# Filling the Q ring of two head pairs by engine copies, and a new order of the first part, in a fused attention and feed-forward kernel

## Chip, cores and metric

The kernel runs on one core of a Trainium2 chip. The metric is the time of one execution on the device in microseconds. In the names of the profile, PE is TensorE (matrix products; PEld are its weight loads), DVE is VectorE, ACT is ScalarE, POOL is GpSimd and SP is SyncE, which here only issues DMAs.

## The reference

The work is a block-sparse causal attention followed by a feed-forward layer. There are 4 batches, 8 heads, 768 positions and a head size of 64.

```
chunk, top_k = 32, 6                      # 24 chunks of 32 keys
k_min, k_max = min and max of k over each chunk
ub  = sum_d max(q * k_min, q * k_max)     # bound of each query on each chunk
ub  = where(chunk is not in the future, ub, -1e9)
sel = the 6 chunks with the highest ub, for each query
scores = q @ k^T / 8, masked by sel and by causality
x   = softmax(scores) @ v                 # heads side by side: (4, 768, 512)
xn  = (x - mean) / sqrt(var + 1e-6) * g
out = x + relu(xn @ w1) @ w2              # hidden size 2048, float32 out
```

## The kernel before

The heads are taken in 16 pairs (numbered g, four for each batch): the two heads of a pair share the 128 partitions, one in the upper and one in the lower half. The 768 positions are six tiles of 128, in two halves of three tiles (r = 0 or 1).

Every step of the work is a small function. A text constant, ORDER, lists all calls by hand, 928 of them. Each engine executes its own instructions strictly in that order; there is no scheduler that could pull something ahead. A step is written as its name and its arguments: smm.5.0.0 is "scores of pair 5, half 0, bin 0". A suffix such as @1 or @2 picks another engine for a step that has several to choose from, or a number of extra products on constants for a step that has such (function busy).

The steps that matter, for a pair g:

- ld, ldb and ldv load q, k and v. Pairs 0 to 3 (batch 0) come in halves and are transposed on PE (turn, line 236); pairs 4 and up are loaded so that VectorE can transpose them (line 229).
- kbound (lines 283 and 284) takes minima and maxima of k by chunk, kdiag and bounds make the bounds, select picks the chunks, maskt and mring bring the mask into the ring.
- qhi and qlo split q in two f16 parts (lines 251 to 256); qrel makes the positive parts (262, 263).
- kcopy and qring write K and Q into ring tiles KA, KB, QA and QB (four of each, so that pair g uses tile g % 4). In one product these give the score and the mask penalty. For pairs 4 and up the Q part is a copy within the on-chip memory, issued as two DMAs of 96 KB from SyncE (lines 267 and 268).
- smm (line 414) are the score products, sexp (422) the exponentials on ScalarE, diag (429) cuts above the diagonal on GpSimd, values (445) multiplies with v, norm and pstat divide by the sum and gather the statistics. The score products write into a pool of two PSUM buffers, which the first feed-forward product shares.

For a batch b and a half r: centre (484 to 487) subtracts the mean, xt transposes by DMA (504), m1 (513) and relu (525) are the first feed-forward product, m2 (538) the second, fin (547, 552) adds x and stores. The weights come in four chunks each, w1 (173) and w2 (177), as DMAs that GpSimd issues and that convert to f16.

Products that compute nothing are there to keep TensorE busy: warm(n) issues n products of 512 columns on a zeroed tile while the first loads are under way (line 373); busy (line 117) issues some on constants ahead of the products of certain steps.

In the part around 60 us SyncE's queue is, in order, the loads of pairs 6 and 7 (ldb.6.kn, ldb.6.qn, ldb.7.kn, ldb.7.qn), then the ring of pair 5 (qring.5), then the transposes of the second half of batch 0 (xt.0.1).

Of the kernel before, what the change touches and what calls it, by code (L numbers as in the profile page):

```python
# [19 lines left out]
def kernel(  # L20
# [10 lines left out]
    nc = tc.nc  # L31
    P = nc.NUM_PARTITIONS
# [9 lines left out]
    HP = H // 2  # L42
# [39 lines left out]
    NK = 4  # L82
    QA = [ring.tile([P, S], F16, name=f"QA{i}", tag=f"QA{i}") for i in range(NK)]
# [24 lines left out]
    def pick(*engines):  # L108
        return engines[min(other[0], len(engines) - 1)]

    def copy(eng, o, i):
        return eng.copy(o, i) if eng is nc.scalar else eng.tensor_copy(o, i)
# [152 lines left out]
    def qring(g, i=None):  # L265
        if i is None:
            nc.sync.dma_start(QA[g % NK][0:64, :], st[g]["qh"][0:64, :])
            nc.sync.dma_start(QB[g % NK][64:P, :], st[g]["qh"][64:P, :])
            return
        qt = st[g]["qn", i]  # L270
        a, z = span(g, i)
        nc.scalar.activation(QA[g % NK][0:64, a * P:z * P], qt[0:64, :], ACTF.Copy, scale=QS)
        nc.scalar.activation(QB[g % NK][64:P, a * P:z * P], qt[64:P, :], ACTF.Copy, scale=QS)
# [269 lines left out]
    def fin(b, r, i, e=None):  # L543
# [13 lines left out]
        consts ld.0.0 rrows.0.0 rinit.0 ld.1.0 ld.2.0 warm.8 turn.0.qn.0 rrows.2.1@1 qpos.0.0 rrows.3.1 qring.0.0  # L557
        turn.0.kn.0 rinit.2 kbound.0.0 rinit.1 turn.1.qn.0 kcopy.0.0 ld.3.0 turn.1.kn.0 kbound.1.0 kdiag.0.0
        qring.1.0 rrows.1.0 rinit.3 turn.2.qn.0@3 ld.0.1 rrows.0.1 bounds.0.0@2 kdiag.1.0 rrows.1.1 qpos.1.0
        select.0.0 turn.2.kn.0 kcopy.2.0@1 kcopy.1.0 qpos.2.0 bounds.1.0@2 kbound.2.0 qring.2.0 maskt.0.0 select.1.0  # L560
        kdiag.2.0 turn.3.kn.0 mring.0.0@1 ld.1.1 turn.3.qn.0 kcopy.3.0 rrows.3.0 ldv.2.0 maskt.1.0 qpos.3.0
        kbound.3.0 smm.0.0.0 ldv.0.0 mring.1.0 bounds.2.0@2 select.2.0 turn.0.kn.1 qring.3.0 rrows.2.0 smm.0.0.1
        turn.1.kn.1 turn.0.qn.1 ld.2.1 kdiag.3.0 sexp.0.0.0 ldv.3.0 kcopy.0.1 qpos.0.1 kbound.1.1 sexp.0.0.1
        kbound.0.1 kcopy.1.1 ldv.1.0 kdiag.0.1 smm.1.0.0@2 bounds.3.0@2 maskt.2.0 diag.0.0 qring.0.1 bounds.0.1
        sexp.1.0.0 select.3.0 values.0.0 maskt.3.0 mring.2.0 kdiag.1.1 smm.1.0.1 select.0.1 smm.2.0.0 w1.2.3 w1.1.3
        w1.0.2 norm.0.0 sexp.1.0.1 ldb.4.qn smm.2.0.1 sexp.2.0.0 mring.3.0 maskt.0.1 ld.3.1 turn.1.qn.1 sexp.2.0.1
        qpos.1.1 ldb.5.kn mring.0.1 diag.1.0 values.1.0 norm.1.0 diag.2.0 pstat.0.0 smm.3.0.0 pstat.1.0
        turn.2.kn.1@1 sexp.3.0.0 kbound.2.1 qring.1.1 turn.4.qn smm.3.0.1@2 sexp.3.0.1 bounds.1.1 values.2.0
        smm.0.1.0 diag.3.0 select.1.1 kcopy.2.1 smm.0.1.2@1 values.3.0 sexp.0.1.0 norm.2.0 sexp.0.1.2 norm.3.0
        turn.2.qn.1 smm.0.1.1 pstat.2.0 sexp.0.1.1 kdiag.2.1@1 qpos.2.1 smm.0.1.3 qring.2.1 ldv.0.1 turn.3.kn.1  # L570
        maskt.1.1 pstat.3.0 qhi.4 kcopy.3.1 mring.1.1 diag.0.1 smm.1.1.0@2 ldb.4.kn bounds.2.1 sexp.1.1.0 sexp.0.1.3
        centre.0.0 xt.0.0.0 xt.0.0.1 select.2.1 turn.3.qn.1@3 kbound.3.1 qlo.4 smm.1.1.3 xt.0.0.2 ldb.5.qn qring.4
        maskt.2.1 turn.4.kn sexp.1.1.3 smm.1.1.2 values.0.1 kdiag.3.1 qpos.3.1 qrel.4 kbound.4 sexp.1.1.2 smm.1.1.1
        bounds.3.1 mring.2.1 sexp.1.1.1 w1.3.3 late select.3.1 kdiag.4 diag.1.1 norm.0.1 turn.5.kn m1.0.0.0 kcopy.4
        turn.5.qn relu.0.0.0 kbound.5 m1.0.0.4 ldv.1.1 qring.3.1 ldb.6.kn relu.0.0.4 w2.0.0 m1.0.0.2 relu.0.0.2
        bounds.4 pstat.0.1 m1.0.0.10 qhi.5 m1.0.0.6 relu.0.0.10 relu.0.0.6 maskt.3.1 kcopy.5@1 kdiag.5 m1.0.0.8
        m1.0.0.12 relu.0.0.8 m1.0.0.14 relu.0.0.12 ldb.6.qn smm.2.1.0 select.4 qlo.5 rstd.0.0 qrel.5 relu.0.0.14
        sexp.2.1.0 bounds.5 smm.2.1.1 smm.2.1.2 ldv.2.1 ldv.3.1 w2.1.0 turn.6.kn sexp.2.1.1 values.1.1 smm.2.1.3
        mring.3.1 diag.2.1 sexp.2.1.2 select.5 sexp.2.1.3 norm.1.1 smm.3.1.0 maskt.4 sexp.3.1.0 smm.3.1.2 kbound.6
        mring.4 maskt.5 w2.2.1 w2.3.1 sexp.3.1.2 smm.3.1.1 ldb.7.kn smm.3.1.3 sexp.3.1.1 ldb.7.qn values.2.1 qring.5  # L580
        sexp.3.1.3 mring.5 pstat.1.1 norm.2.1 smm.4.1.0 diag.3.1 sexp.4.1.0 smm.4.0.0 kdiag.6 values.3.1 m2.0.0.0.0
        norm.3.1 pstat.2.1 pstat.3.1 smm.5.0.0 kcopy.6 sexp.4.0.0 sexp.5.0.0 m2.0.0.2.0 m2.0.0.1.0 smm.4.0.1
        m2.0.0.0.1 sexp.4.0.1 turn.6.qn qhi.6 centre.0.1 qlo.6 smm.4.1.3 turn.7.kn smm.4.1.2 sexp.4.1.3 sexp.4.1.2
        m2.0.0.1.1 turn.7.qn qrel.6 smm.4.1.1 rstd.0.1 m2.0.0.2.1 kcopy.7 kbound.7 m2.0.0.0.2 m2.0.0.2.2 sexp.4.1.1
        m2.0.0.1.2 smm.5.1.0 xt.0.1.0 bounds.6 m2.0.0.2.3 select.6 xt.0.1.1 xt.0.1.2 ldb.8.kn sexp.5.1.0 qhi.7
        m1.0.1.0 qlo.7 diag.4.0 ldv.4 turn.8.kn qring.6 m1.0.1.6 relu.0.1.0 relu.0.1.6 m2.0.0.0.3 m1.0.1.14 ldb.8.qn
        kdiag.7 fin.0.0.0 qrel.7 fin.0.0.2 relu.0.1.14 ldb.9.qn diag.4.1 m1.0.1.2 kbound.8 maskt.6 ldv.5 relu.0.1.2
        ldv.6 kcopy.8 ldb.10.qn m2.0.0.1.3 qring.7 turn.8.qn mring.6 m1.0.1.4 relu.0.1.4 diag.5.0 m1.0.1.8 qhi.8
        relu.0.1.8 ldv.7 fin.0.0.1 values.4.0 norm.4.0 smm.5.0.1 bounds.7 qlo.8 smm.5.1.1 qrel.8 select.7 sexp.5.0.1
        kdiag.8 sexp.5.1.1 smm.5.1.3 values.4.1 diag.5.1 sexp.5.1.3 smm.5.1.2 ldb.9.kn values.5.0 ldb.10.kn  # L590
        ldb.12.qn sexp.5.1.2 smm.6.1.0 sexp.6.1.0 bounds.8 norm.4.1 smm.6.1.2 norm.5.0 values.5.1 sexp.6.1.2
        smm.6.1.1 sexp.6.1.1 pstat.4.1 m2.0.1.0.0 m1.0.1.10 qring.8 m1.0.1.12 m2.0.1.0.1 relu.0.1.10 relu.0.1.12
        smm.6.0.0 sexp.6.0.0 turn.9.qn maskt.7 select.8 smm.6.0.1 sexp.6.0.1 m2.0.1.0.2 pstat.4.0 maskt.8 smm.6.1.3
        qhi.9@1 diag.6.0 m2.0.1.0.3 mring.7 pstat.5.0 norm.5.1 fin.0.1.0 smm.7.0.0 diag.6.1 sexp.6.1.3 sexp.7.0.0
        smm.7.0.1 values.6.1 diag.7.0 values.6.0 mring.8 sexp.7.0.1 norm.6.1 smm.7.1.0 smm.7.1.2 values.7.0 qlo.9
        m2.0.1.2.0 norm.6.0 norm.7.0 sexp.7.1.0 smm.7.1.3 sexp.7.1.2 m2.0.1.1.0 pstat.6.0 pstat.7.0 smm.7.1.1
        ldb.11.kn sexp.7.1.3 m2.0.1.1.1 sexp.7.1.1 diag.7.1 turn.9.kn centre.1.0 xt.1.0.0 smm.8.1.0 m2.0.1.2.1
        sexp.8.1.0 smm.8.0.0 m2.0.1.2.2 kbound.9 m2.0.1.1.2 smm.8.1.2 m2.0.1.2.3 xt.1.0.2 kcopy.9 qrel.9 sexp.8.0.0
        values.7.1 sexp.8.1.2 smm.8.0.1 pstat.6.1 xt.1.0.1 smm.8.1.3 sexp.8.0.1 norm.7.1 sexp.8.1.3 kdiag.9 diag.8.1
        ldb.11.qn pstat.5.1 m2.0.1.1.3 smm.8.1.1 fin.0.1.2 bounds.9 pstat.7.1 centre.1.1 sexp.8.1.1 xt.1.1.0  # L600
        m1.1.0.0 m1.1.0.2 relu.1.0.0 xt.1.1.1 m1.1.0.4 relu.1.0.2 m1.1.0.6 relu.1.0.4 relu.1.0.6 m1.1.0.8 relu.1.0.8
        xt.1.1.2 m1.1.0.14 relu.1.0.14 m1.1.0.10 m1.1.0.12 relu.1.0.10 turn.10.qn relu.1.0.12 ldv.8 ldv.10 select.9
        turn.10.kn kbound.10 fin.0.1.1 maskt.9 m1.1.1.0 qhi.10@1 ldv.9 qring.9 kdiag.10 qlo.10 m1.1.1.4 rstd.1.0
        qrel.10 mring.9 kcopy.10 turn.11.kn values.8.1 bounds.10 select.10 relu.1.1.0 smm.9.0.0 turn.11.qn
        m2.1.0.0.0 norm.8.1 ldb.12.kn relu.1.1.4 smm.9.1.0 sexp.9.0.0 m2.1.0.0.1 smm.9.0.1 sexp.9.1.0 sexp.9.0.1
        kbound.11 m2.1.0.1.0 m2.1.0.0.2 diag.8.0 smm.9.1.3 sexp.9.1.3 m2.1.0.0.3 qhi.11 qring.10 ldv.13 maskt.10
        qring.11 mring.10 smm.9.1.2 sexp.9.1.2 values.8.0 smm.9.1.1 sexp.9.1.1 kdiag.11 m2.1.0.1.1 m1.1.1.14
        m2.1.0.1.2 kcopy.11 relu.1.1.14 fin.1.0.0 smm.10.0.0 ldv.11 qlo.11 m2.1.0.1.3 diag.9.1 qrel.11 turn.12.qn
        bounds.11 sexp.10.0.0 m1.1.1.2 m1.1.1.8 ldb.13.kn turn.12.kn relu.1.1.2 fin.1.0.1 select.11 rstd.1.1
        m1.1.1.6 relu.1.1.8@1 norm.8.0 maskt.11 values.9.1 mring.11 smm.10.0.1 relu.1.1.6 smm.10.1.0 qhi.12  # L610
        kbound.12 norm.9.1 sexp.10.0.1 m2.1.0.2.0 diag.9.0 smm.10.1.3 values.9.0 m2.1.0.2.1 sexp.10.1.0 smm.10.1.1
# [79 lines left out]
```

## Time and profile before

| | before |
|---|---|
| time, median of 3 runs | 288.89 us (288.71 to 291.12) |
| span of the profiled execution | 288.7 us, 6793 instructions |
| PE busy | 271.7 us (94%) |
| VectorE busy | 211.8 us (73%) |
| ScalarE busy | 180.8 us (63%) |
| GpSimd busy | 94.1 us (33%) |
| DMA | 32.42 MB, mean 112 GB/s |
| chain that ended last | PE 81%, DMA 8%, VectorE 7%, ScalarE 2% |

Busy shares are means over the whole span. The profile also gives them by 40 slices, with the TensorE clock that was granted, and by any stretch one asks for. The chain is followed back from the last instruction, at each step to what released it.

### The profile page before, as it was taken

What the parts mean: (1) busy time and instruction counts of PE and PEld (TensorE: products, weight loads), DVE (VectorE), ACT (ScalarE), POOL (GpSimd) and SP (SyncE); (2) the same over time, 40 slices, a digit from 0 to 9 for tenths busy, and PEclk for the clock granted to TensorE, in tenths of its full rate; (3) what the DMA queues carried; (4) which work ended last, traced back from release to release, by engine and by line L of the source; (5) the groups of instructions that cost most, each with busy time, mean ns of one, the idle gap of its engine ahead of it and who ended that gap; (6) DMA issues with size and microseconds to landing.
All of it is one profiled execution on the core that took longest, in us unless ns stands there. A gap on an engine that the chain in (4) does not pass through costs nothing.

```text
span 288.7 us, 6793 instructions
## 1 busy us (share of the span) xinstructions
PE 271.7 (94%) x2628; PEld 181.8 (63%) x2628; DVE 211.8 (73%) x629; ACT 180.8 (63%) x241; POOL 94.1 (33%) x165
## 2 busy tenths in 40 slices
PE   5999999992799999999899999999999999999994
PEld 2889997671355777566656776566667745555541
DVE  5699999998079998999699979998797483221212
ACT  3688999694185977865775877667777522513210
POOL 8505615781039203182442643141072200100100
PEclk9999999998599999999999999999999999999999
DMA  6999997999949989489919691927011112310102
GB/s 141 203 179 177 202 156 126 167 151 194 139 84 70 188 162 182 78 116 133 172 29 185 112 148 20 136 81 163 16 43 59 39 20 72 93 39 36 73 0 110
DMA packets 136063, 32.42 MB, mean 112 GB/s; under 512 B 127072, under 2 KB 132960, under 8 KB 136032
## 3 DMA queue, kind: packets, MB, share of 16 engines
q1 hardware_dynamic: 106640, 24.39, 43.7%
q0 software_dynamic: 29248, 7.34, 27.4%
q8 instruction: 20, 0.33, 0.5%
q10 hardware_dynamic: 144, 0.26, 0.4%
q14 instruction: 11, 0.09, 0.1%
HBM read 27.53 MB, written 6.29 MB: 117 GB/s over the span
## 4 chain that ended last, share of the span: by engine, by line
PE 81%; DMA 8%; DVE 7%; ACT 2%; issue 1%; ACTq 0%; DVEq 0%
PE yp L538 27%; PE mm L513 25%; PE mm L414 11%; PE sm L445 6%; DMA QA<-q 3%; PE ub L333 3%; DMA xT<-xc 3%; PE ub L320 2%; ACT pt L422 2%; PE tr L236 2%; DMA raw<-in_k_dram 2%; PE tr L117 2%; DVE xc L487 1%; PE trh L361 1%; PE ub L117 1%; PE mm L117 1%
## 5 line engine op out<-in xcount | busy, mean ns | idle before, releaser
L422 ACT ACTIVATE pt<-mm 128x1024 f16<-128x1024 f32 (+2 forms) x96 | 84.6, 917 | 30.0 <-PE mm L414 28.9
L538 PE MATMUL yp<-w2b,hT 128*128 128x512 f16 (+2 forms) x400 | 94.8, 377 | 0.0
L513 PE MATMUL mm<-xT,w1b 128*128 128x384 f16 x512 | 87.9, 326 | 0.8 <-DMA xT<-xc 0.8
L525 ACT ACTIVATE hT<-mm 128x768 f16<-128x768 f32 x61 | 49.1, 810 | 59.0 <-PE mm L513 58.8
L513 PEld LDWEIGHTS <-w1b 128*128 128x128 f16 x512 | 49.5, 98 | 34.5 <-issue 0.9
L538 PEld LDWEIGHTS <-hT 128*128 128x128 f16 x400 | 38.0, 99 | 34.9 <-issue 2.1
L429 POOL TENSOR_SCALAR_AFFINE_SELECT pt<-pt 128x768 f16<-128x768 f16 x32 | 27.9, 878 | 46.6 <-ACT pt L422 46.6
L414 PE MATMUL mm<-QA,KA 128*128 128x128 f16 (+2 forms) x224 | 34.3, 248 | 8.4 <-DMA QA<-q 7.5
L547 DVE SCALAR_TENSOR_TENSOR ot<-yp,rstd,x 128x512 f32<-128x512 f32 (+2 forms) x25 | 17.9, 721 | 31.7 <-PE yp L538 18.5
L414 PE MATMUL mm<-QB,KB 128*128 128x128 f16 (+2 forms) x224 | 34.4, 248 | 0.0
L498 POOL TENSOR_TENSOR rstd<-ve,mhalf 128x3 f32<-128x3 f32 x8 | 7.0, 875 | 70.9 <-DVE ve L495 70.8
L414 PEld LDWEIGHTS <-KA 128*128 128x128 f16 x224 | 17.9, 98 | 16.5 <-DMA QA<-q 8.0
L445 PEld LDWEIGHTS <-pt 128*128 128x128 f16 x672 | 24.4, 98 | 2.3
L445 PE MATMUL sm<-va,pt 128*128 128x65 f16 x672 | 25.4, 193 | 0.0
L303 POOL TENSOR_TENSOR kc<-kc 128x24 f32<-128x24 f32 x12 | 6.2, 513 | 54.9 <-DVE kc L284 54.8
L414 PEld LDWEIGHTS <-KB 128*128 128x128 f16 x224 | 18.1, 99 | 4.4 <-issue 1.3
L475 DVE BATCH_NORM_STATS2 bst<-x 128x6 f32<-128x128 f32 x96 | 20.3, 276 | 0.0
L460 DVE TENSOR_TENSOR x<-sm,rden 128x384 f32<-128x384 f32 x32 | 17.8, 558 | 1.1
L256 DVE SCALAR_TENSOR_TENSOR q<-qnT,q 128x640 f16<-128x640 f32 x12 | 9.9, 828 | 10.1 <-ACT q L253 10.0
L487 DVE SCALAR_TENSOR_TENSOR xc<-x,mv,gall 128x512 f16<-128x512 f32 x24 | 16.7, 750 | 0.2 <-DMA xT<-xc 0.2
L206 POOL DMA_DIRECT2D va<-in_v_dram x12 | 12.8, 1064 | 0.0
L213 POOL DMA_DIRECT2D va<-in_v_dram x16 | 12.7, 795 | 0.0
(95 smaller groups left out, 347.8 us busy)
## 6 DMA issues: line engine op xcount, KB each, us to landing
out_dram<-ot SPq DMA_DIRECT2D x23, 256.0 KB, 2.3
qnb<-in_q_dram SPq DMA_DIRECT2D x48, 96.0 KB, 2.7
knb<-in_k_dram SPq DMA_DIRECT2D x48, 96.0 KB, 3.0
va<-in_v_dram POOLq DMA_DIRECT2D x12, 192.0 KB, 5.9
w1b<-in_moe_w_ch_dram POOLq DMA_DIRECT2D x4, 512.0 KB, 7.2
w2b<-in_moe_w_ch_dram POOLq DMA_DIRECT2D x4, 512.0 KB, 8.4
raw<-in_k_dram SPq DMA_DIRECT2D x16, 96.0 KB, 3.9
raw<-in_q_dram SPq DMA_DIRECT2D x16, 96.0 KB, 3.9
```

What stands on the lines that cost most here:

```text
L206: nc.gpsimd.dma_start(va[:, :, :, 0:D].rearrange("p h t d -> p (h t) d"), v[b, 2 * hp:2 * hp + 2].rearrange("h (t p) d -> p (h t) d", p=P),)
L414: nc.tensor.matmul(sc[:, hh, o:o + w * P], ks[:, t * P:(t + 1) * P], qs[:, s * P:(s + w) * P], start=True, stop=True,)
L422: nc.scalar.activation(st[g]["pt", r][:, 4 * i:4 * i + o].rearrange("p n h x -> p h n x"), st[g]["sc", r, i][:, :, 0:o * P].rearrange("p h ...
L429: nc.gpsimd.affine_select(out=dv, in_=dv, compare_op=ALU.is_ge, fill=0.0, base=0, pattern=[[0, 2 * TR], [1, P]], channel_multiplier=-1,)
L445: nc.tensor.matmul(pv[:, hh, s2, :], pt[:, where[t, s], hh, :], va[:, hh, t, 0:D + 1], start=(t == 0), stop=(t == s),)
L460: nc.vector.tensor_tensor(xh(b, r)[:, :, 2 * hp:2 * hp + 2, :].rearrange("p s h d -> p h s d"), pv[:, :, :, 0:D], rden.to_broadcast([P, 2, ...
L475: nc.vector.bn_stats(half(b, r)["st"][:, i, hp], xh(b, r)[:, i, 2 * hp:2 * hp + 2].rearrange("p h d -> p (h d)"),)
L487: nc.vector.scalar_tensor_tensor(h["xc"][:, i, :], xs, h["mv"][:, i, 0:1], gall, op0=ALU.subtract, op1=ALU.mult,)
L513: nc.tensor.matmul(hp_[:, i, 0:TR * P], w1b[:, kt, (m + i) * P:(m + i + 1) * P], h["xT"][:, kt], start=(kt == 0), stop=(kt == KT1 - 1),)
L525: nc.scalar.activation(h["hT"][:, m:m + 2], h["hp", m][:, :, 0:TR * P], ACTF.Relu, scale=HS)
L538: nc.tensor.matmul(h["yp", i][:, cs], h["hT"][:, kt, i * P:(i + 1) * P], w2b[:, kt, cs], start=(kt == 0), stop=(kt == KT2 - 1),)
L547: nc.vector.scalar_tensor_tensor(ot[:, cs], h["yp", i][:, cs], h["rstd"][:, i:i + 1], xh(b, r)[:, i].rearrange("p h d -> p (h d)")[:, cs], ...
```

## The change

The change has three parts. The Q ring of pairs 4 and 5 is no longer filled by DMAs but by copies on an engine; as the engine is chosen by the suffix, pair 4 (no suffix) is copied by VectorE and pair 5 (@2) by GpSimd. Three more products on constants run ahead of the first loads. And the first part of ORDER, up to about the middle of the list, is written in a new order, with some steps on other engines; the last 299 steps are as before. The rings of pairs 6 and up remain DMAs.

It is for taking these two rings off the DMA queue, and for fitting the steps around them anew.

```diff
     def qring(g, i=None):
+        if HP <= g < HP + 2:
+            eng = pick(nc.vector, nc.scalar, nc.gpsimd)
+            copy(eng, QA[g % NK][0:64, :], st[g]["qh"][0:64, :])
+            copy(eng, QB[g % NK][64:P, :], st[g]["qh"][64:P, :])
+            return
         if i is None:
             nc.sync.dma_start(QA[g % NK][0:64, :], st[g]["qh"][0:64, :])
             nc.sync.dma_start(QB[g % NK][64:P, :], st[g]["qh"][64:P, :])
...
     ORDER = """
-        consts ld.0.0 rrows.0.0 rinit.0 ld.1.0 ld.2.0 warm.8 turn.0.qn.0 rrows.2.1@1 qpos.0.0 rrows.3.1 qring.0.0
-        turn.0.kn.0 rinit.2 kbound.0.0 rinit.1 turn.1.qn.0 kcopy.0.0 ld.3.0 turn.1.kn.0 kbound.1.0 kdiag.0.0
-        qring.1.0 rrows.1.0 rinit.3 turn.2.qn.0@3 ld.0.1 rrows.0.1 bounds.0.0@2 kdiag.1.0 rrows.1.1 qpos.1.0
+        consts ld.0.0 warm.11 rrows.2.1@1 rrows.0.0 ld.1.0 rinit.3 turn.0.qn.0 rrows.3.1 rinit.1 rinit.2 rinit.0
+        turn.0.kn.0 turn.1.qn.0@1 qpos.0.0 rrows.0.1 ld.2.0 kbound.0.0 ld.3.0 turn.1.kn.0 kdiag.0.0 ld.1.1 qring.0.0
+        kcopy.0.0 kbound.1.0 qpos.1.0 rrows.1.0 bounds.0.0@2 turn.2.qn.0@3 qring.1.0 kdiag.1.0 ldv.2.0 rrows.1.1
...
-        mring.3.1 diag.2.1 sexp.2.1.2 select.5 sexp.2.1.3 norm.1.1 smm.3.1.0 maskt.4 sexp.3.1.0 smm.3.1.2 kbound.6
-        mring.4 maskt.5 w2.2.1 w2.3.1 sexp.3.1.2 smm.3.1.1 ldb.7.kn smm.3.1.3 sexp.3.1.1 ldb.7.qn values.2.1 qring.5
-        sexp.3.1.3 mring.5 pstat.1.1 norm.2.1 smm.4.1.0 diag.3.1 sexp.4.1.0 smm.4.0.0 kdiag.6 values.3.1 m2.0.0.0.0
-        norm.3.1 pstat.2.1 pstat.3.1 smm.5.0.0 kcopy.6 sexp.4.0.0 sexp.5.0.0 m2.0.0.2.0 m2.0.0.1.0 smm.4.0.1
+        diag.2.1 w2.1.0 turn.6.kn smm.2.1.3 sexp.2.1.2 sexp.2.1.3 select.5 w2.2.1 smm.3.1.0 sexp.3.1.0 kbound.6
+        smm.3.1.2 smm.3.1.1 norm.1.1 maskt.5 ldb.6.qn ldb.7.kn mring.4 mring.5 qring.5@2 sexp.3.1.2 smm.3.1.3
+        sexp.3.1.1 values.2.1 sexp.3.1.3 pstat.1.1 smm.4.1.0 diag.3.1 values.3.1 sexp.4.1.0 norm.2.1 norm.3.1
+        smm.4.0.0 smm.5.0.0 pstat.2.1 pstat.3.1 sexp.4.0.0 m2.0.0.0.0 smm.4.0.1 w2.3.1 sexp.5.0.0 turn.6.qn kcopy.6
...
```

Steps with another suffix in the new order: kcopy.0.1@1 (VectorE instead of ScalarE), mring.2.1@1 (ScalarE instead of VectorE), kdiag.3.1@1 (GpSimd instead of VectorE), qhi.7@1, qhi.11@1 and qhi.12@1 (VectorE instead of ScalarE), qhi.10 (ScalarE instead of VectorE), kcopy.9@1 (GpSimd instead of ScalarE), turn.1.qn.0@1 and values.0.1@1 (eight products on constants each, none before), smm.0.1.2 (none, four before).

## Prediction

> **What bounds the kernel now.** I read the slices of the page first: one row per engine, 40 slices of 7.2 us, each digit the busy share in tenths.
>
> ```profile
> PE   5999999992799999999899999999999999999994
> ...
> DVE  5699999998079998999699979998797483221212
> ...
> PEclk9999999998599999999999999999999999999999
> DMA  6999997999949989489919691927011112310102
> ```
>
> TensorE is full nearly everywhere. There is one hole, in the tenth slice (65 to 72 us), where PE falls to 2 tenths. VectorE falls to 0 one slice later, and TensorE's granted clock to 5 tenths, while the DMA engines are at 9 tenths. Next, the costliest groups (busy us, mean ns | idle before, releaser), for who ends that hole:
>
> ```profile
> L414 PE MATMUL mm<-QA,KA 128*128 128x128 f16 (+2 forms) x224 | 34.3, 248 | 8.4 <-DMA QA<-q 7.5
> ```
>
> Of 8.4 us of waiting before this group, 7.5 are one wait for a DMA into the Q ring. The timeline of 55 to 82 us (start, length, instruction, idle before it) has it:
>
> ```profile
> 64.57 3.00 SPq L267 DMA_DIRECT2D QA<-q  x1
> ...
> 67.67 1.24 SPq L268 DMA_DIRECT2D QB<-q  x1
> ...
> 74.19 0.61 PE L414 MATMUL mm<-QA,KA 128*128 128x128 f16 x4 [7.49 <-DMA QA<-q]
> ...
> 75.02 3.62 PE L538 MATMUL yp<-w2b,hT 128*128 128x512 f16 x8
> ...
> 80.60 0.82 DVE L256 SCALAR_TENSOR_TENSOR q<-qnT,q 128x640 f16<-128x640 f32 x1 [9.58 <-ACT q L253]
> ```
>
> The scores of pair 5 (smm.5.0.0) stand at the head of PE's in-order queue until 74.19. The ring copy was issued at 64.57 and landed 9.6 us later. ScalarE then waited for PE (7.09 us), VectorE for ScalarE (9.58). The issues to DMA between 58 and 66 us (last number: us to landing) say why it was late:
>
> ```profile
> w2b<-in_moe_w_ch_dram POOLq DMA_DIRECT2D x3, 512.0 KB, 8.7
> qnb<-in_q_dram SPq DMA_DIRECT2D x4, 96.0 KB, 9.6
> ...
> QA<-q SPq DMA_DIRECT2D x1, 96.0 KB, 9.6
> ```
>
> Three weight chunks went out just before it; over the whole run the median Q-ring landing is 2.5 us. Last, busy time by stage (PE, PEld, DVE, ACT, POOL, clock, DMA share, GB/s):
>
> ```profile
> 40.00:50.00 10.00, 10.00 (x123) 7.81 (x121) 9.85 (x25) 9.69 (x15) 3.76 (x8) 1.00 0.87 137
> 50.00:60.00 10.00, 9.76 (x112) 6.77 (x110) 9.73 (x39) 7.62 (x10) 8.06 (x14) 1.00 1.28 155
> 60.00:70.00 10.00, 6.32 (x108) 4.87 (x106) 9.69 (x28) 7.74 (x9) 5.37 (x11) 0.97 1.26 172
> 70.00:80.00 10.00, 5.81 (x22) 2.84 (x23) 1.02 (x2) 1.90 (x3) 0.00 (x0) 0.52 0.98 150
> 80.00:90.00 10.00, 10.00 (x79) 5.83 (x77) 8.29 (x22) 7.65 (x9) 5.48 (x11) 1.00 0.64 79
> ```
>
> So there are three regimes: up to 65 us VectorE (9.7 of 10 us) sets the pace, with ScalarE close, and PE's fill is partly products on constants; 66 to 80 is the hole; after it PE is full with real products to the end.
>
> **What the skill says.** The Trainium skill, "TensorE: Matmul & The Clock Gate", Part 1: after an idle window of about 3.4 us TensorE runs at half rate until a busy one has passed. The trace agrees: after the 7.5 us pause, 512-column products start every 0.43 us instead of 0.216. "DMA: Bandwidth & Descriptors", "Issuing engines are not separate DMA queues": copies issued by different engines share 16 DMA engines and interleave; 9.6 against 2.5 us is how that looks here. "VectorE: DVE Perf Modes", the TRN2 errata section, prices an SBUF copy at 58 + N/4 cycles of 0.96 GHz in the fastest mode: 0.26 us for 768 columns, an estimate. "SBUF — State Buffer", "SBUF: two separate sides": a VectorE operation on two ports and a GpSimd one exclude each other for a whole instruction; no row here isolates that, though L303 on GpSimd goes from 0.24 (median) to 1.72 us at worst.
>
> **The change, part by part.**
>
> *Rings of pairs 4 and 5.* Four DMAs (2 x 96 KB each pair) leave SyncE's queue. Pair 4 becomes two copies of 64x768 f16 on VectorE; pair 5, marked @2, goes to GpSimd, not VectorE. The nearest VectorE row is the 128x640 f16 L262, 0.32 us; with the 0.26 of the skill as low end and 0.61 (slowest 64x384 KB<-RT) as high end I take 0.37, 0.7 us for both. It is done near 44 us, 20 us before smm.4.1.0. GpSimd: L112 casts 64x768 in 0.83 us; two make 1.7 us (3.4 if each waits as long again for the shared ports). GpSimd's order is now diag.2.1, two w2 issues, these copies, diag.3.1, the last w2 issue. diag.2.1 can start when sexp.2.1.0 ends (57.98), not behind the v loads as before (60.60): 58.9 after 0.9 us, 61.4 after two w2 issues of 1.25, 63.1 after the copies. smm.5.0.0 comes at about 65.6 (below), so the copies are hidden by 2.5 us, or 0.8 at the high end. Queued behind them: diag.3.1, done at 64.0, for which values.3.1 waits (64.65 before), no loss; and the last w2 chunk, out at about 65.4 instead of 63.2.
>
> *What the hole gives back.* Idle: 7.5 us. Half rate: 8 products of L538 took 3.4 instead of 1.73 us (1.7), 8 of L414 1.04 instead of 0.45 (0.6), the next L538 and L414 about 0.5. Together 10.3 us.
>
> *What takes some of it.* PE without the wait: smm.4.1.0 at 63.8, values.3.1 to 65.1, smm.4.0.0, smm.5.0.0 to 66.0 (its PSUM buffer comes free with sexp.4.1.0 at 65.6), three steps to 68.2; m2.0.0.0.1 needs w2's second chunk: issued 60.2, 8.7 us to land: 68.9, a wait of 0.7. The third chunk lands at 70.2, PE asks at 72; the fourth at 74, PE asks near 79. m1.0.1.0 comes up near 77.6. It needs the transposed xT: centre.0.1 ends at 71 as before, its last DMA goes out at about 72 (before 74.5, behind the ring DMAs) and takes 4.3 us, up to 8: 76 to 80; I take 0.5 us of wait. In the kernel before m1.0.1.0 started at 87.6 with two more m2 steps (0.86 each) done: comparable time 85.9. Gain 85.9 - 77.6 = 8.3, less 0.5: 7.8 us.
>
> *First loads and products.* Eight warm products run from 1.84 to 5.26 at 0.427 us; PE then sits until q lands at 6.55. Three more last 1.28 us: to 6.54, exactly the pause. Cost nothing; their use is that the clock gate sees no pause: the transposes at 6.55 and 8.28 took 1.5 us per six, later ones 0.66. Up to 1.5 us earlier on PE; VectorE, which follows, gets perhaps 0.7.
>
> *The new first part.* VectorE gains kcopy.0.1 (0.54 + 0.56) and the copies (0.7), loses mring.2.1 (0.7) and kdiag.3.1 (0.24): +0.9 before the hole. Against it: rinit and rrows.0.1, 1.1 us of work, now stand in VectorE's idle time before the first kbound (1.6 us idle at 6.5). ScalarE: +0.7 to 1.0 for mring.2.1, -0.95 for kcopy.0.1. Sum near zero; with the earlier clock I take 0.8 us of gain, between -1.0 and +1.8. qhi.7 on VectorE costs 0.57 where VectorE sat idle. The remaining moves are swaps of neighbours; the eight products each for turn.1.qn.0 and values.0.1 (0.7 and 0.45 us), less four at smm.0.1.2, lie in PE's slack before 45 us. From about 176 us the orders are identical, and PE-bound, so nothing is lost later.
>
> Sum: 7.8 + 0.8 = 8.6 us; 288.9 - 8.6 = 280.3.
>
> **The rivals.** *All of it* (0.17): w2 and xT arrive in time, the front gains its most: 10.3 + 1.5, 277.1. For: four DMAs fewer on a crowded queue. Against: the second w2 chunk has no slack by the sum above. *The DMA engines are the bound* (0.13): the share is 1.26 up to 70 us; w2 or xT keeps PE waiting some 4 us in the ring's place, long enough for half rate again: 7.5 - 4 = 3.5 us gained, 285.4. Against: at 80 to 90 us the share falls to 0.64, so there was room. *Slower* (0.06): GpSimd copies at 3.4 us and locked against VectorE push diag.3.1 and the last w2 issue back; PE stops as long at values.3.1 and m2 as it did at the ring, and the 2.4 us added to VectorE (0.7 + 1.1 + 0.6), the pace up to 65 us, come on top: about 291.3. The profile's POOL idle after 66 us speaks against it.
>
> **Chances.** Forecast 0.64, 280.3; the rivals as given. Half of the DMA case lies within 1% (above 286.0): faster 0.87, same 0.07, slower 0.06. The range 276.5 to 285.0 takes in the first rival, the forecast with the front's ends, and part of the second.
>
> **What would show it.** Right: no wait of PE for QA or QB of several us; no slice of clock at 5 tenths; no VectorE hole at 71 us; m1.0.1.0 (the second stretch of L513) near 77; GpSimd rows of QA<-q around 0.83 us near 62; first transposes still at about 6.55 but shorter. Wrong: a wait of over 3 us before L538 on w2b or before L513 on xT between 66 and 82 us; GpSimd copies well over 1 us; diag.3.1 releasing PE; VectorE's first centre later than 37 us.

## The result, and the profile after

The changed kernel takes 280.45 us (median of 4 runs, 280.19 to 282.44) against 288.80 for the kernel before (4 runs, 288.70 to 291.12): 0.971 of the time, 95% interval 0.964 to 0.977. In the later measurements below the kernel before scattered between 280.8 and 293.0 us (56 runs in four sets, medians 288.3 to 289.5, 14 of them under 285), and where a set has such short runs, the kernels below gain only 0 to 2% on those alone, so the medians of all runs, which are given, measure mainly how the long runs go away.

The line numbers of the changed kernel are 5 higher below qring: L267 is now L272, L414 L419, L513 L518, L538 L543. The slices of the changed kernel's page:

```profile
PE   7989998999999999999999999999999999999994
DVE  6888999899999989999999989898876665021212
...
PEclk9999999999999999999999999999999999999999
DMA  6989999989999995699614799455021012210202
```

The hole of the tenth slice is gone on all three rows: PE is at 9, VectorE has no 0 before the last fifth, and the granted clock never leaves 9. The DMA row is as full as it was up to there, so the transfers were not made cheaper; PE no longer waits there for one of them. The score group of the same page:

```profile
L419 PE MATMUL mm<-QA,KA 128*128 128x128 f16 (+2 forms) x224 | 34.0, 246 | 0.9 <-ACT pt L427 0.7
```

Its idle time fell from 8.4 to 0.9 us, and what ends most of it is now ScalarE (0.7), not the DMA. The timeline of 62 to 67 us shows the new supplier of pair 5's ring:

```profile
62.48 0.83 POOL L112 COPY QA<-q 64x768 f16<-64x768 f16 x1
...
63.37 0.82 POOL L112 COPY QB<-q 64x768 f16<-64x768 f16 x1
...
64.27 0.86 POOL L434 TENSOR_SCALAR_AFFINE_SELECT pt<-pt 128x768 f16<-128x768 f16 x1
...
66.98 0.39 PE L419 MATMUL mm<-QA,KA 128*128 128x128 f16 x4
```

GpSimd ends the ring at 64.2 and diag.3.1 at 65.1; PE comes to smm.5.0.0 at 66.98, without a wait. By stage (PE, PEld, DVE, ACT, POOL, clock, DMA share, GB/s):

```profile
40.00:50.00 10.00, 8.67 (x101) 6.70 (x99) 9.89 (x26) 8.27 (x12) 6.12 (x13) 1.00 1.21 174
...
60.00:70.00 10.00, 9.13 (x145) 6.83 (x141) 9.74 (x36) 9.27 (x12) 7.61 (x16) 1.00 1.04 146
70.00:80.00 10.00, 10.00 (x77) 5.73 (x76) 9.86 (x27) 7.96 (x10) 4.88 (x9) 1.00 1.42 166
```

From 60 to 80 us PE does 19.1 us of work in place of 12.1, VectorE 19.6 in place of 10.7. One stage got worse: from 40 to 50 us PE fell from 10.0 to 8.7. The timeline of PE names it, the first feed-forward product:

```profile
45.93 4.06 PE L518 MATMUL mm<-xT,w1b 128*128 128x384 f16 x24 [1.33 <-DMA xT<-xc]
```

Before, it started at 44.71 and did not wait:

```profile
44.71 4.14 PE L513 MATMUL mm<-xT,w1b 128*128 128x384 f16 x24
```

### The profile page after: what moved, and what is told of

Read it like the earlier page. It is cut to its first block, busy times and chain, and to the rows that moved or that the text cites. A ratio compares the mean times of both kernels' runs of the same rounds, so it can differ in the third digit from the quotient of the medians.

```text
span 278.8 us, 6816 instructions
## 1 busy us (share of the span) xinstructions
PE 269.2 (97%) x2643; PEld 180.1 (65%) x2643; DVE 215.9 (77%) x632; ACT 177.9 (64%) x237; POOL 99.4 (36%) x170
## 4 chain that ended last, share of the span: by engine, by line
PE 87%; DVE 6%; DMA 3%; ACT 2%; issue 1%; SPq 1%; DVEq 0%; ACTq 0%
PE mm L518 30%; PE yp L543 30%; PE mm L419 11%; PE sm L450 6%; PE ub L325 3%; DMA xT<-xc 2%; PE junk L378 2%; PE trh L366 1%; ACT pt L427 1%; PE tr L236 1%; PE ub L338 1%; PE ub L117 1%; DVE bst L480 1%; PE tr L117 1%; DVE x L465 1%; DMA raw<-in_q_dram 1%
## 5 line engine op out<-in xcount | busy, mean ns | idle before, releaser
L543 PE MATMUL yp<-w2b,hT 128*128 128x512 f16 (+2 forms) x400 | 93.0, 370 | 0.0
L518 PE MATMUL mm<-xT,w1b 128*128 128x384 f16 x512 | 88.3, 326 | 1.3 <-DMA xT<-xc 1.3
L518 PEld LDWEIGHTS <-w1b 128*128 128x128 f16 x512 | 49.4, 98 | 34.9 <-issue 1.4
L543 PEld LDWEIGHTS <-hT 128*128 128x128 f16 x400 | 37.3, 98 | 33.2
L434 POOL TENSOR_SCALAR_AFFINE_SELECT pt<-pt 128x768 f16<-128x768 f16 x32 | 29.9, 940 | 50.5 <-ACT pt L427 50.3
L419 PE MATMUL mm<-QA,KA 128*128 128x128 f16 (+2 forms) x224 | 34.0, 246 | 0.9 <-ACT pt L427 0.7
L419 PE MATMUL mm<-QB,KB 128*128 128x128 f16 (+2 forms) x224 | 34.0, 246 | 0.0
L419 PEld LDWEIGHTS <-KA 128*128 128x128 f16 x224 | 18.1, 98 | 9.7 <-issue 1.4
L308 POOL TENSOR_TENSOR kc<-kc 128x24 f32<-128x24 f32 x12 | 4.8, 402 | 50.0 <-DVE kc L289 47.9
L419 PEld LDWEIGHTS <-KB 128*128 128x128 f16 x224 | 17.9, 98 | 3.8 <-issue 0.4
L492 DVE SCALAR_TENSOR_TENSOR xc<-x,mv,gall 128x512 f16<-128x512 f32 x24 | 17.6, 785 | 1.2 <-DMA xT<-xc 1.2
L213 POOL DMA_DIRECT2D va<-in_v_dram x16 | 12.7, 795 | 0.0
L206 POOL DMA_DIRECT2D va<-in_v_dram x12 | 12.7, 1058 | 0.0
L256 DVE SCALAR_TENSOR_TENSOR q<-qnT,q 128x640 f16<-128x640 f32 x12 | 10.8, 899 | 2.0 <-ACT q L253 1.9
```

The costliest lines, as they stand in the source:

```text
L206: nc.gpsimd.dma_start(va[:, :, :, 0:D].rearrange("p h t d -> p (h t) d"), v[b, 2 * hp:2 * hp + 2].rearrange("h (t p) d -> p (h t) d", p=P),)
L419: nc.tensor.matmul(sc[:, hh, o:o + w * P], ks[:, t * P:(t + 1) * P], qs[:, s * P:(s + w) * P], start=True, stop=True,)
L434: nc.gpsimd.affine_select(out=dv, in_=dv, compare_op=ALU.is_ge, fill=0.0, base=0, pattern=[[0, 2 * TR], [1, P]], channel_multiplier=-1,)
L492: nc.vector.scalar_tensor_tensor(h["xc"][:, i, :], xs, h["mv"][:, i, 0:1], gall, op0=ALU.subtract, op1=ALU.mult,)
L518: nc.tensor.matmul(hp_[:, i, 0:TR * P], w1b[:, kt, (m + i) * P:(m + i + 1) * P], h["xT"][:, kt], start=(kt == 0), stop=(kt == KT1 - 1),)
L543: nc.tensor.matmul(h["yp", i][:, cs], h["hT"][:, kt, i * P:(i + 1) * P], w2b[:, kt, cs], start=(kt == 0), stop=(kt == KT2 - 1),)
```

## The experiments

All times are medians. None of these kernels leaves out work.

**The kernel before once more**, for a second profile.

> The kernel before, unchanged, for a second profile. Both theories: near 288.8 us, with the pause of PE for the ring of pair 5 (6 to 8 us, ending near 74 us) and the slice at half clock behind it. If the pause were an accident of one execution, it would be absent or under 3 us here.

It took 289.44 us. The waits of PE between 30 and 100 us (total, times, longest):

```profile
PE mm L414 <- DMA QA<-q: 7.6, 1, 7.6
```

So the pause is not an accident of one execution. It need not be in every one: both profiles are of long executions (290.76 and 289.44 us).

**Only the ring copies, in the old order.**

```diff
     def qring(g, i=None):
+        if HP <= g < HP + 2:
+            eng = pick(nc.vector, nc.scalar, nc.gpsimd)
+            copy(eng, QA[g % NK][0:64, :], st[g]["qh"][0:64, :])
+            copy(eng, QB[g % NK][64:P, :], st[g]["qh"][64:P, :])
+            return
...
-        ... ldb.7.qn values.2.1 qring.5
+        ... ldb.7.qn values.2.1 qring.5@2
```

> The kernel before with only the ring copies (pair 4 on VectorE, pair 5 on GpSimd), old order, eight warm products. Theory A (the late ring DMA is the loss, and any ring that is filled in time recovers it): the copies run at 63.9 to 65.6 us on GpSimd and push diag.3.1 to 66.5, so PE waits about 1.9 us before values.3.1 in place of 7.5, and no half clock: 280 to 282 us. Theory B (the new order carries the gain, the copies alone only move the wait to w2 or to GpSimd): 286 us or more.

It took 281.63 us (280.88 to 282.57): theory A. Its timeline has the forecast wait, in kind and size:

```profile
66.48 0.86 POOL L434 TENSOR_SCALAR_AFFINE_SELECT pt<-pt 128x768 f16<-128x768 f16 x1
...
67.39 0.99 PE L450 MATMUL sm<-va,pt 128*128 128x65 f16 x27 [1.87 <-POOL pt L434]
```

values.3.1 waits for diag.3.1, which stands behind the two copies on GpSimd.

**Only the new order, rings by DMA.** The changed kernel without the five added lines of qring.

> The changed kernel with rings 4 and 5 put back to DMAs, all else new. Theory A, as to where the DMA stands: the ring of pair 5 is now issued near 58 us, ahead of the second and third w2 chunk (60.5, 61.7), so it lands by 62 to 66 us, before PE asks at 66.5: 280 to 282 us, the copies add next to nothing to the new order. Theory B' (the copies themselves carry it; a ring DMA in this crowd lands late wherever it is issued): lands after 70 us, PE waits over 3 us, half clock again, 285 us or more.

It took 282.48 us (20 runs, 280.70 to 285.56). PE has no wait for QA or QB in its profile. SyncE's queue there (timeline) issues the ring before the weights of 59.85 and 61.11 can crowd it:

```profile
55.48 2.46 SPq L194 DMA_DIRECT2D knb<-in_k_dram  x4
58.46 0.47 SPq L267 DMA_DIRECT2D QA<-q  x1
59.04 0.52 SPq L268 DMA_DIRECT2D QB<-q  x1
59.66 6.04 SPq L194 DMA_DIRECT2D qnb<-in_q_dram  x4
```

It landed early, as theory A has it (issues to DMA between 58 and 59.5 us):

```profile
QA<-q SPq DMA_DIRECT2D x1, 96.0 KB, 3.3
QB<-q SPq DMA_DIRECT2D x1, 96.0 KB, 2.9
```

So most of the gain is there without a copy. The median is 0.5 us outside the expected band and 2 above the changed kernel. In its profile 1 us of that lies between smm.2.1.0 and m1.0.1.0 (21.52 us for 20.56), where PE waited 0.54 us for VectorE; the rest was not traced.

**The old order with one step moved**: the same two DMAs, ahead of pair 7's loads.

```diff
-        mring.4 maskt.5 w2.2.1 w2.3.1 sexp.3.1.2 smm.3.1.1 ldb.7.kn smm.3.1.3 sexp.3.1.1 ldb.7.qn values.2.1 qring.5
+        mring.4 maskt.5 w2.2.1 w2.3.1 sexp.3.1.2 smm.3.1.1 qring.5 ldb.7.kn smm.3.1.3 sexp.3.1.1 ldb.7.qn values.2.1
```

> The kernel before with one step moved: qring.5, still two DMAs, ahead of ldb.7.kn in SyncE's queue (issue near 53 to 56 us in place of 64.6). Theory A: lands by 62 us, no wait at smm.5.0.0, no half clock, loads of pair 7 some 1.2 us later: 279 to 281.5 us. Theory B' (lands late wherever it is issued): over 3 us of wait for QA or QB, 285 us or more.

It took 280.42 us (278.76 to 281.57), as good as the whole change. The issues to DMA between 51 and 54 us (last number: us to landing), and its page's clock row:

```profile
QA<-q SPq DMA_DIRECT2D x1, 96.0 KB, 7.4
QB<-q SPq DMA_DIRECT2D x1, 96.0 KB, 6.8
```

```profile
PEclk9999999999999999999999999999999999999998
```

The transfer is hardly faster (7.4 us against 9.6), but it starts at 51.9 in place of 64.6 and has landed nearly 8 us before PE asks at 67.1. A slow transfer that is asked for late enough cost nothing here.

**The changed kernel once more**, for its scatter.

> The changed kernel, unchanged, on the chip where the kernel before spread from 281.05 to 292.96 us over 23 runs. Theory A (the spread of the kernel before is the length of the pause, that is, when the ring DMA happens to land): the changed kernel has no such wait and stays within 280 to 283. Theory S (the spread belongs to the chip or to the weight DMAs in general): it spreads over 8 us or more too.

It took 280.01 us (279.33 to 282.07), the kernel before beside it 288.44 (286.54 to 290.66): theory A, as far as six runs tell. The scatter of the kernel before goes with the granted clock: each execution on record has its mean granted clock beside its time, and this mean is 0.991 to 1.000 in the eight shortest of the 56 (under 283 us), 0.976 to 0.991 in the 40 of 286.5 us and more, and 0.981 and 0.985 in the two profiled ones, which have the pause. That the short ones have a short pause or none is argued from this; none of them was profiled.

The profile is of the longest of the six. In it the wait for xT in the first feed-forward product is 1.76 us, and this time the clock fell (timeline of PE to 48 us, then the page's clock row):

```profile
45.92 2.40 PE L518 MATMUL mm<-xT,w1b 128*128 128x384 f16 x7 [1.76 <-DMA xT<-xc]
```

```profile
PEclk9999997999999999999999999999999999999999
```

**The warm products.** The early ring with 11 for 8, and the changed kernel with 8 for 11.

```diff
-        consts ld.0.0 rrows.0.0 rinit.0 ld.1.0 ld.2.0 warm.8 turn.0.qn.0 rrows.2.1@1 qpos.0.0 rrows.3.1 qring.0.0
+        consts ld.0.0 rrows.0.0 rinit.0 ld.1.0 ld.2.0 warm.11 turn.0.qn.0 rrows.2.1@1 qpos.0.0 rrows.3.1 qring.0.0
```

> The kernel before with the ring DMA of pair 5 early and 11 warm products for 8. Theory W (the three products open the clock earlier and the front moves up): first transposes 0.8 us per six for 1.5, and 0.3 to 0.8 us less than with the early ring alone: 279.6 to 280.1. Theory N (the front is paced by the loads and by VectorE): shorter transposes, but the same time within 0.3 us of 280.4.

> The changed kernel with 8 warm products for 11. Theory W: transposes at 1.5 us per six again and 0.3 to 0.8 us more than the changed kernel. Theory N: the same within 0.3 us.

They took 282.49 us (280.06 to 283.90) and 281.13 (278.96 to 285.01). The first is 2 us above the early ring alone, where theory W has a gain; the second is 1.1 above the changed kernel, as W has it; and each range overlaps that of the kernel it is held against: no gain is measured. The first transposes of the changed kernel with 8 products, after the pause that the extra three would fill:

```profile
6.54 0.85 PE L236 MATMUL tr<-ident_f,raw 128*128 128x128 f32 x6 [1.09 <-DMA raw<-in_q_dram]
```

They are nearly as short as with 11 products (0.82 to 0.84 in all seven profiles of kernels with 11). With 8 products three of seven profiles have 0.85 and four 1.51. So the extra products do go with short transposes, which 8 products get in some executions only. That this shortens the whole was not seen. The profile of the early ring with 11 (283.66 us, one of its longer executions) is 1.5 us ahead of the early ring alone at centre.0.0 (35.22 for 36.77), as W has it, and loses the lead at 44.08: VectorE had waited 2.64 us for a k load, PE 2.37 us for VectorE, and a stretch at half rate followed.

**The old order, copies behind diag.3.1.** With the five added lines of qring, as above.

```diff
-        ... ldb.7.qn values.2.1 qring.5
-        ... smm.4.1.0 diag.3.1 sexp.4.1.0 ...
+        ... ldb.7.qn values.2.1
+        ... smm.4.1.0 diag.3.1 qring.5@2 sexp.4.1.0 ...
```

> The old order with the ring copies, those of pair 5 behind diag.3.1 on GpSimd instead of ahead of it. Theory A: the 1.9 us that PE waited for GpSimd's diag at values.3.1 goes, the copies run from about 65.4 to 67.1 us and end as the first m2 step does (smm.5.0.0 comes after it); wait 0 to 0.6: 279.5 to 280.8 us, one to two us under the copies ahead of diag.3.1. Rival (the copies only move the wait along the queue of GpSimd): PE waits 1.5 us or more at smm.5.0.0 and the time stays at 281.6.

It took 280.72 us (278.80 to 282.04) against 281.63 ahead of diag.3.1, and PE's wait for L434 is gone from its list of waits, with none for QA or QB in its place. The two ranges overlap; the wait is what decides: from smm.2.1.0 to m1.0.1.0 its profile takes 21.47 us, that of the copies ahead of diag.3.1 23.25.

**The weights later.** Issues of w2's third and fourth chunk behind kdiag.6.

```diff
-        mring.4 maskt.5 w2.2.1 w2.3.1 sexp.3.1.2 ...
+        mring.4 maskt.5 sexp.3.1.2 ...
...
-        ... smm.4.0.0 kdiag.6 values.3.1 ...
+        ... smm.4.0.0 kdiag.6 w2.2.1 w2.3.1 values.3.1 ...
```

> The kernel before with the issues of the third and fourth w2 chunk behind kdiag.6 on GpSimd (about 67 and 68 us in place of 62 and 63); the ring of pair 5 stays the same two DMAs at the same place in SyncE's queue. Theory C (the weight chunks in flight are what makes the ring late): it lands 3 to 6 us after its issue in place of 9.6 to 11, PE's wait for it falls under 4 us; later m2 steps wait for w2 instead, so the time itself may not fall. Theory Q (the loads of pair 7 ahead of it on the same queue are what makes it late): it still lands about 9 us after its issue, PE's wait stays at 6 us or more.

They went out at 64.35 and 65.64, only some 2.5 us later, as GpSimd was done sooner. The issues to DMA between 58 and 70 us of this kernel, then its longest wait of PE:

```profile
QA<-q SPq DMA_DIRECT2D x1, 96.0 KB, 6.7
QB<-q SPq DMA_DIRECT2D x1, 96.0 KB, 5.4
```

```profile
PE mm L414 <- DMA QA<-q: 2.5, 1, 2.5
```

The ring lands in 6.7 us for 9.6 and 11.2 in the two profiles of the kernel before, and the wait falls from 7.5 to 2.5; one run took 284.82 us. That is theory C's direction and its bound on the wait, though not quite its landing time. The other profiles say the same. When the ring of pair 5 went out, no weight chunk was in flight with the new order and DMAs (3.3 us to land), one in this kernel (6.7) and one with the early ring (7.4), three in the two profiles of the kernel before (9.6 and 11.2; in the second the last of the three went out 0.1 us behind the ring). The loads of pair 7 do not sort these cases: the k loads went out just ahead of the ring of 3.3 us, and none of pair 7's ahead of the ring of 7.4. These are five executions of kernels that differ in more than this, so it is an ordering and not a law.

**The v load of pair 3 behind w1.** In the changed kernel ldv.3.1 stands ahead of the last w1 chunk.

```diff
-        mring.1.1 qpos.2.1 qring.2.1 smm.1.1.0@2 centre.0.0 qhi.4 sexp.1.1.0 bounds.2.1 kcopy.3.1 ldv.3.1
+        mring.1.1 qpos.2.1 qring.2.1 smm.1.1.0@2 centre.0.0 qhi.4 sexp.1.1.0 bounds.2.1 kcopy.3.1
...
-        ... m1.0.0.14 ldv.2.1 qlo.5 qrel.5 mring.3.1
+        ... m1.0.0.14 ldv.2.1 ldv.3.1 qlo.5 qrel.5 mring.3.1
```

> The changed kernel with ldv.3.1 (the v load of pair 3, second half) behind ldv.2.1 as in the old order, so that the last w1 chunk goes out 1.6 us sooner, clear of the transposes of xT that start at 38.1 us. Theory X (the 1.3 to 1.8 us that PE waits for xT in the changed kernel's first part is this collision): xT lands 1 us or more sooner, the wait falls under 0.5 us, and the time by about 1 us, to 279.0 (280.0 before on this chip). Rival (first part paced elsewhere): the wait for xT falls but ScalarE or VectorE is reached right behind it, time within 0.3 us of 280.0.

> The changed kernel with ldv.3.1 behind ldv.2.1, a second time. Theory X (the collision of xT with the last w1 chunk was worth about 1 us): no wait for xT in the first part, 278.8 to 279.6 us again, against 280.0 and 280.45 for the changed kernel in its two measurements. Rival (the 279.34 was the chip of that measurement): 279.8 to 280.5.

It took 279.34 us (278.90 to 280.25) and 279.52 (279.10 to 282.43), the best of all kernels here. The last w1 chunk, issued at 37.93 in the changed kernel, goes out sooner (timeline of GpSimd), and the first product has no wait (timeline of PE):

```profile
35.16 0.79 POOL L173 DMA_DIRECT2D w1b<-in_moe_w_ch_dram  x1 [0.30 <-POOL w1b L172]
```

```profile
43.23 1.46 PE L518 MATMUL mm<-xT,w1b 128*128 128x384 f16 x8
```

Theory X for the wait, though part of it moves on, as the rival has it: the second m1 step now waits 0.36 and 0.71 us for ScalarE in the two profiles. The medians are 0.5 to 1.1 us below the changed kernel's 280.01 and 280.45, which is of the forecast size, but the ranges overlap, and that 280.01 was not measured on the chip of either of these two. In the profiles both are ahead at smm.2.1.0 (55.01 and 55.29, against 55.99 to 58.74 in the five other profiles of this order), yet at least 0.5 us of the lead was there at centre.0.0 (35.29 and 35.21 against 35.84 to 36.50) and had begun long before the moved step acts (first exponential at 18.52 us in both, at 18.71 to 19.29 in the five). How much of the time is the collision's was not separated.

**The ring of pair 5 on VectorE.**

```diff
-        smm.3.1.2 smm.3.1.1 norm.1.1 maskt.5 ldb.6.qn ldb.7.kn mring.4 mring.5 qring.5@2 sexp.3.1.2 smm.3.1.3
+        smm.3.1.2 smm.3.1.1 norm.1.1 maskt.5 ldb.6.qn ldb.7.kn mring.4 mring.5 qring.5 sexp.3.1.2 smm.3.1.3
```

> The changed kernel with the ring of pair 5 copied by VectorE, as pair 4 is, and not by GpSimd. From pair 4's copies (0.50 and 0.45 us) VectorE gains 0.95 us near 65 us, GpSimd loses 1.7 ahead of diag.3.1. Theory P (VectorE is the pace there): centre.0.1 and with it xT end 1 us later, 280.3 to 281.0. Rival (GpSimd's queue is the tighter one, since diag.3.1 and the last w2 chunk stand behind the copies): 279.0 to 279.7.

It took 281.07 us (280.80 to 282.62), 0.6 to 1.1 above the changed kernel's two medians: theory P's direction and band, with overlapping ranges. Its profile shows only part of the mechanism. The copies took VectorE 0.34 and 0.36 us; centre.0.1 comes 13.3 us after smm.2.1.0 in place of 12.5, but PE does not wait for xT behind it, and m1.0.1.0 comes 20.86 us after smm.2.1.0 in place of 20.56. The rest of the difference was not traced.

## Why the prediction was right

The forecast was 280.3 us, and 280.45 was measured. The mechanism held: the late ring was the loss. That the sum came so close is in part luck, as its terms were off in both directions.

- *The hole* was worth what its lines say. The waits for ring, ScalarE and VectorE and the half-rate stretch went together. That it was the late ring, and not the order, is shown from two sides: copies in the old order give 281.6 (280.7 behind diag.3.1), the same DMAs issued 12.7 us earlier give 280.4.
- *GpSimd's copies*: 0.83 us each, as forecast; start 62.5, end 64.2 against 61.4 and 63.1. They were hidden, and diag.3.1 and the last w2 issue (65.57 against 65.4) came in time. *Pair 4's copies* took 0.50 and 0.45 us in place of 0.37.
- *What takes some of it* was too large, and one reading in it was wrong. I set off two m2 steps that the kernel before had done ahead of m1.0.1.0. By the two ORDER texts, and by the products counted in the profiles (40 and 36 of line 538, in the changed kernel 543), it is one step, 0.86 us: the comparable time was 86.7 and not 85.9. The waits of 0.7 us for w2's second chunk and 0.5 for xT did not come either. From smm.2.1.0 to m1.0.1.0 the kernel before took 31.54 us (56.04 to 87.58) and the changed one 20.56 (57.19 to 77.75): less one m2 step a gain of 10.1 us, forecast 7.8, and close to the 10.3 that the hole's own lines add up to. The old order reaches the same with the early ring (21.48 us) and with the copies behind diag.3.1 (21.47), against 21.42 for the changed kernel with the m2 step added.
- *The new first part*: I took a gain of 0.8 us. In the two profiles up to centre.0.0 there is one, 0.56 us (36.50 for 37.06), but the last w1 chunk, moved from 35.6 to 37.9 us by the v loads put ahead of it, now goes out beside the xT transposes of 38.1. They land in 5.6 us for 3.3, PE waits 1.33 us at 45.93, and the part ends 1.15 us behind. I had called the remaining moves swaps of neighbours. The same fault as the one being mended, a transfer that PE needs put beside a weight chunk, went unseen in its smaller form; putting ldv.3.1 back takes the wait away. The 1.15 us themselves are within the scatter: smm.2.1.0 comes at 55.75 to 56.65 in six of seven profiles of the old order and at 55.99 to 58.74 in the five of the new one that have ldv.3.1 ahead. No gain of the new first part is shown.
- *The warm products* do fill a pause without cost, but what they were to earn was not seen in the time.
- *Nothing is lost later* held: from the product at 176.81 us (186.48 before) both kernels take 102 us to the end. Between m1.0.1.0 and that product, a stretch that the sum put at nothing, the kernel before takes 98.90 us and the changed one 99.06, with one m2 step of 0.86 us more to do. The 0.7 us gained are about the wait of 0.8 us for xT at 138 us that only the kernel before has.

So 10.1 - 1.15 + 0.7 = 9.7 us up to there, where the forecast had 8.6. The difference of the two profiled spans, 288.7 and 278.8, is larger than the 8.35 us between the medians: the profiled execution of the kernel before took 290.76 us, 2 over its median.

The rivals: a wait for xT came, but at 46 us and not between 66 and 82, and with 1.33 us. No half rate followed in that profile; in the repeat of the changed kernel it did, after 1.76 us. The slower case had no support, as GpSimd's copies ran at their price beside VectorE's.

## What to carry to other kernels

Where an in-order engine stands for microseconds at one DMA, first look what was issued just ahead of it and how early its source was ready; moving the issue ahead of the bulk loads may do all that a replacement by copies does, for no engine time. If copies are used, put them behind what the critical engine waits for next (here this took away a wait of 1.87 us), and rather on the engine with slack, for which the evidence here is weaker. When an order is rewritten, check each transfer that the critical engine needs against every bulk load that moved, however neighbourly the move looks.

## What the runs showed of the hardware

A 96 KB copy within the on-chip memory took 2.5 us in the median of a whole run. For the ring of pair 5 it was 3.3 us with no weight chunk of 512 KB in flight at its issue, 6.7 and 7.4 with one, 9.6 and 11.2 with three (one of them issued 0.1 us later in the second case).

TensorE's clock fell to half after pauses well under the 3.4 us that the prediction takes for an idle window: after 1.76 us (the changed kernel once more), 2.37 (early ring with 11 warm products) and 2.47 (the weights later). It did not after 1.33 us (the changed kernel) and 1.87 (only the ring copies). As 1.76 us was enough and 1.87 was not, the length of the pause did not decide alone.

The change from half to full clock at the start came at different points in executions with the same eight warm products: the first six transposes took 1.51 us in four profiles and 0.85 in three.
